# k^T v as four full-array products, y in 32-column quads, A and y issued together, more transposes by DMA

## The chip, the cores and the metric

The kernel runs on one core of one Trainium2 chip. The metric is device time of the whole program in microseconds (us), lower is better. Each profile also records the span from the first instruction to the last, which is about 1.8 us shorter than the time of the same execution, and the clock that TensorE was granted (1.00 is full speed).

Engine names in the profile: PE is TensorE's matmuls, PEld its weight loads, DVE is VectorE, ACT is ScalarE, POOL is GpSimd, SPq the queue of SyncE that issues DMA.

## The reference, cut to what matters

A gated linear recurrence over 768 steps, for 4 batches of 8 heads of width 48, feeds a two-layer network:

```python
for t in range(S):
    state = alpha[:, :, t, :, None] * state + einsum('bhd,bhe->bhde', k[:, :, t], v[:, :, t])
    y[:, :, t] = einsum('bhd,bhde->bhe', q[:, :, t], state)
x = y.transpose(0, 2, 1, 3).reshape(3072, 384)
h = x @ w_in                       # 384 -> 2048
out = (s * relu(h)**2 + b) @ w_out # 2048 -> 384
```

## The kernel before

The sequence is cut into 24 blocks of 128 steps, 6 for each batch. Heads go in pairs. For each block TensorE computes the cumulative log gates (`st_cum`), transposes of scaled q and k (`st_T`, or a DMA transpose), the block's contribution to the state (k^T v, `st_KV`), the causal score matrix A (`st_A`, masked by VectorE) and the output y (`st_y`). Two large matmuls, `mm1` with w_in and `mm2` with w_out, follow for groups of 2 or 4 blocks. A small list scheduler in the kernel puts all of this in one fixed order for each engine, from durations and priorities. Where this plan leaves TensorE idle, the kernel issues dummy matmuls on zeros (`fill`): 41 in the kernel before, all before 36 us. They count as busy time.

k^T v used half the array's columns at a time, and y a mix of 64-column pairs (m = 2) and 32-column quads (m = 1):

```python
def st_KV(n):
    kb = qk_sb[n % 3][:, 1].rearrange("a h d -> a (h d)")
    vp = vp_sb[n % 4]              # [v of head 0 | zeros | v of head 1], 48 columns each
    for p in range(NP):
        for e in range(2):
            nc.tensor.matmul(
                out=p_ps[64 * e : 64 * e + 64, p, :],
                lhsT=kb[:, 128 * p + 64 * e : 128 * p + 64 * e + 64],
                rhs=vp[:, p, 48 * e : 48 * e + 96], start=True, stop=True)

Y_PARTS = [   # pair of heads, state (None) or head, first 32-column piece, pieces
    (0, None, 0, 2), (2, None, 6, 2), (1, None, 4, 2), (3, None, 10, 2),
    (0, 0, 0, 2), (2, 0, 6, 2), (1, 1, 4, 2), (3, 1, 10, 2),
    (2, None, 8, 1), (3, None, 9, 1), (0, None, 2, 1), (1, None, 3, 1),
    (2, 1, 8, 1), (3, 0, 9, 1), (0, 1, 2, 1), (1, 0, 3, 1),
    (1, 0, 4, 1), (0, 1, 1, 1), (3, 0, 10, 1), (2, 1, 7, 1)]

def st_y(n):
    # ... cut: start flags, and blocks without a state leave out the None parts
    nc.tensor.matmul(
        out=y_ps[32 * (x % 4) : 32 * (x % 4) + 32 * m, x // 4, :],
        lhsT=st[:, p, c0 : c0 + 32 * m] if e is None else vp[:, p, c0 + 48 * e : ...],
        rhs=qT[:, p, :] if e is None else am[:, e, p, :], ...)
```

The inputs of the blocks and the weight quarters load through one queue, in this order (b: the four inputs of a block; i and o: a quarter of w_in and of w_out). After o3 has landed, its cast and a column sum, TensorE computes one bias product:

```python
LOADS = ["b0", "b1", "i0", "b2", "i1", "i2", "b3", "i3", "b4", "o0", "b5", "o1", "o2", "b6", "o3"]
```

Of the kernel before, what the change touches and what calls it, by code (L numbers as in the profile page):

```python
# [9 lines left out]
BF16 = mybir.dt.bfloat16  # L10
AF = mybir.ActivationFunctionType
ALU = mybir.AluOpType
# [3 lines left out]
VW = 144  # L16

GROUPS = [2, 2, 2, 2, 4, 4, 4, 4]
LEAD = {1: 20.0, 2: 20.0, 4: 29.0}

NPE = 14

RING = 12

NST = 4

LOADS = ["b0", "b1", "i0", "b2", "i1", "i2", "b3", "i3", "b4", "o0", "b5", "o1", "o2", "b6", "o3"]

class Schedule:

# [97 lines left out]
def kernel(  # L128
# [12 lines left out]
    nc = tc.nc  # L141
    ctx.enter_context(tc.manual_schedule())

    B, H, S, D = q.shape
    C = 128
    NCH = S // C
    NP = H // 2
    NBLK = B * NCH
# [3 lines left out]
    NIN = 5  # L152
# [16 lines left out]
    def many(name, n, shape, dtype, zero=None):  # L169
        tiles = []  # L170
        for i in range(n):
            t = sb.tile(shape, dtype, name=f"{name}{i}")
            if zero is not None:
                zero.memset(t, 0.0)
            tiles.append(t)
        return tiles
# [35 lines left out]
    qkT_sb = many("qkT", 3, [128, 2, NP, 128], BF16)  # L212
    am_sb = many("am", 2, [128, 2, NP, 128], BF16)
    blast_sb = many("blast", 2, [128, NP], BF16)
    t1_sb = many("t1", 2, [128, NP, 96], BF16)
    s_sb = many("s_st", 2, [128, NP, 96], BF16)
    xd_sb = many("xd", 3, [128, 3, 512], BF16)
    r_sb = many("r", 2, [128, 512], BF16)
    gt_sb = [sb.tile([128, RING * C], BF16, name=f"gt{j}") for j in range(NJ)]
# [128 lines left out]

    def st_KV(n):
        kb = qk_sb[n % 3][:, 1].rearrange("a h d -> a (h d)")  # L350
        vp = vp_sb[n % 4]
        for p in range(NP):
            for e in range(2):
                nc.tensor.matmul(  # L354
                    out=p_ps[64 * e : 64 * e + 64, p, :],
                    lhsT=kb[:, 128 * p + 64 * e : 128 * p + 64 * e + 64],
                    rhs=vp[:, p, 48 * e : 48 * e + 96],
                    start=True,
                    stop=True,
                )  # L360

    def st_Tcopy(n):
        nc.vector.tensor_copy(
# [1 line left out]
            in_=t_ps.rearrange("a x p t -> a (x p t)"),  # L365
        )

    def st_t1(n):
        bl = blast_sb[n % 2].unsqueeze(2).to_broadcast([128, NP, 96])
        if n % NCH == NCH - 1:  # L370
            return
        if n % NCH == 0:
            nc.vector.tensor_tensor(out=s_sb[n % 2], in0=p_ps, in1=bl, op=ALU.mult)
        else:
            nc.vector.tensor_tensor(  # L375
                out=t1_sb[n % 2], in0=p_ps, in1=s_sb[(n - 1) % 2], op=ALU.add
            )

    def st_snew(n):
        if n % NCH in (0, NCH - 1):  # L380
            return
        bl = blast_sb[n % 2].unsqueeze(2).to_broadcast([128, NP, 96])
        nc.gpsimd.tensor_tensor(out=s_sb[n % 2], in0=t1_sb[n % 2], in1=bl, op=ALU.mult)  # L383

    def st_A(n):
        qkT = qkT_sb[n % 3]
# [10 lines left out]
    def st_mask(n):  # L397
# [8 lines left out]




    Y_PARTS = [  # L410
        (0, None, 0, 2), (2, None, 6, 2), (1, None, 4, 2), (3, None, 10, 2),
        (0, 0, 0, 2), (2, 0, 6, 2), (1, 1, 4, 2), (3, 1, 10, 2),
        (2, None, 8, 1), (3, None, 9, 1), (0, None, 2, 1), (1, None, 3, 1),
        (2, 1, 8, 1), (3, 0, 9, 1), (0, 1, 2, 1), (1, 0, 3, 1),
        (1, 0, 4, 1), (0, 1, 1, 1), (3, 0, 10, 1), (2, 1, 7, 1),
    ]

    def st_y(n):
        first = n % NCH == 0
        qT = qkT_sb[n % 3][:, 0]  # L420
        am = am_sb[n % 2]
        vp = vp_sb[n % 4]
        st = s_sb[(n - 1) % 2]
        parts = [x for x in Y_PARTS if not (first and x[1] is None)]
        fresh = {0, 1, 2, 3}
        for i, (p, e, x, m) in enumerate(parts):
            c0 = 32 * x - 96 * p


            mine = {(x + y) % 4 for y in range(m)}  # L430
            start = mine <= fresh
            fresh -= mine
            nc.tensor.matmul(  # L433
                out=y_ps[32 * (x % 4) : 32 * (x % 4) + 32 * m, x // 4, :],
                lhsT=(
                    st[:, p, c0 : c0 + 32 * m]
                    if e is None
                    else vp[:, p, c0 + 48 * e : c0 + 48 * e + 32 * m]
                ),
                rhs=qT[:, p, :] if e is None else am[:, e, p, :],  # L440
                start=start,
                stop=(i >= len(parts) - 4),
            )

    blk_group = []
    for g, m in enumerate(GROUPS):
# [76 lines left out]
    sched = Schedule()  # L523
    op = sched.op
    NG = len(GROUPS)
    UNIT = 1.65

    def first(n):
        return n % NCH == 0

    def last(n):
        return n % NCH == NCH - 1

    def want(n):
        g, t = blk_group[n]
        return (4 * n - LEAD[GROUPS[g]]) * UNIT

# [29 lines left out]
    op("PE", 1.3, -10, bias_mm, r=["bones", "colsum"], w=[("o", 1)], lat=0.27)  # L567
    op("DVE", 0.53, -300, bias_copy, r=[("o", 1)], w=["bias"])

    unit_i = quad_i = 0  # L570
    for g in range(NG):
        m = GROUPS[g]
        ring = [(first_blk[g] + x) % RING for x in range(m)]
        for n in range(first_blk[g], first_blk[g] + m):
            i2, i3, ii = n % 2, n % 3, n % NIN
            t = want(n)
            if n:
                rank = loads.index(f"b{n}") - 1000
                for x, (name, src, dst) in enumerate(
                    (("a", alpha, a_in), ("q", q, q_in), ("k", k, k_in), ("v", v, v_in))  # L580
                ):
                    op("SP", 0.98, rank + 0.1 * x, load, n, src, dst, w=[(name, ii)], lat=2.0)
            op("ACT", 0.45, t - 1.0, st_ln, n, r=[("a", ii)], w=[("la", i2)])
            op("PE", 0.3, t, st_cum, n, r=[("la", i2)], w=["ct"], lat=0.27)
            op("ACT", 0.4, t + 0.1, st_exp_b, n, r=["ct"], w=[("b", i2)])
            op("ACT", 0.55, t + 0.1, st_exp_i, n, r=["ct"], w=[("bi", i2), ("bl", i2)])
            op("POOL", 0.6, t + 0.2, st_vcast, n, r=[("v", ii)], w=[("vp", n % 4)])
            op("DVE", 0.47, t + 0.2, st_qb, n, r=[("q", ii), ("b", i2)], w=[("qb", i3)])
            op("DVE", 0.47, t + 0.2, st_kb, n, r=[("k", ii), ("bi", i2)], w=[("kb", i3)])
            if n < NPE:  # L590
                op("PE", 0.5, t + 0.3, st_T, n, r=[("qb", i3), ("kb", i3)], w=["ct"], lat=0.27)
                op("DVE", 0.61, t + 0.4, st_Tcopy, n, r=["ct"], w=[("qkT", i3)])
            else:
                op("ACT", 0.8, t + 0.3, st_Tdma, n, r=[("qb", i3), ("kb", i3)],
                   w=[("qkT", i3)], lat=5.0)
            op("PE", 0.34, t + 0.35, st_KV, n, r=[("kb", i3), ("vp", n % 4)], w=["py"], lat=0.27)
            if first(n):
                op("DVE", 0.48, t + 0.5, st_t1, n, r=["py", ("bl", i2)], w=[("S", i2)])
            elif not last(n):
                op("DVE", 0.48, t + 0.5, st_t1, n, r=["py", ("S", 1 - i2)], w=[("t1", i2)])  # L600
                op("POOL", 0.9, t + 0.1, st_snew, n, r=[("t1", i2), ("bl", i2)], w=[("S", i2)])
            op("PE", 0.33, t + 0.5, st_A, n, r=[("qkT", i3)], w=["a"], lat=0.27)
            op("DVE", 1.15, t + 0.6, st_mask, n, r=["a"], w=[("am", i2)])
            rr = [("am", i2), ("qkT", i3), ("vp", n % 4)] + ([] if first(n) else [("S", 1 - i2)])
            op("PE", 0.55, t + 0.7, st_y, n, r=rr, w=["py"], lat=0.27)
            op("ACT", 0.43, t + 0.8, st_yevac, n, r=["py"], w=[("xd", g % 3, blk_group[n][1])])
        per = 4 // m
        for u in range(NJ // per):
            w = unit_i
            unit_i += 1  # L610
            js = units[w][1]
            t = w * UNIT
            op("PE", 0.85 if m == 1 else 0.69, t, mm1, w,
               r=[("xd", g % 3, x) for x in range(m)] + [("wib", js[0] // 4)],
               w=[("h", w % 2)], lat=0.27)
            op("ACT", 0.5, t + 0.5, relu, w, r=[("h", w % 2)], w=[("r", w % 2)])
            op("DVE", {1: 0.54, 2: 0.4, 4: 0.335}[m], t + 1.0, square, w, r=[("r", w % 2)],
               w=[("gt", x, j) for j in js for x in ring])
        for u in range(4 * m):
            x = quad_i  # L620
            quad_i += 1
            tt, jq = quads[x][1:]
            ob = (x // 4) % 2
            t = (x + 4 * m + 1.4) * UNIT
            op("PE", 0.67, t, mm2, x,
               r=[("gt", ring[tt], j) for j in range(4 * jq, 4 * jq + 4)] + [("wob", jq)],
               w=[("o", ob)], lat=0.27)
            if jq == 3:
                op("DVE", 0.54, t + 0.1, oevac, x, r=[("o", ob), "bias", "s"],
                   w=[("os", (x // 4) % 3)])  # L630
                op("SP", 0.7, -2000, ostore, x, r=[("os", (x // 4) % 3)])



# [38 lines left out]
```

## Time and profile before

| | before |
|---|---|
| time, median of the first 3 runs | 207.42 us (206.22 to 207.78) |
| span of the profiled run (a fourth one, 208.12 us), clock | 206.3 us, 1.00 |
| TensorE busy, whole span | 185.6 us (90%) |
| bias product starts | 57.12 us |
| last w_out matmul ends | 202.62 us |

First, the profile page's table of 40 equal slices (tenths of busy time in each slice) of the kernel before:

```profile
PE   1979497797599999999999999999999999999992
...
PEclk9999999999999999999999999999999999999999
```

TensorE has holes in the first 11 slices (to 57 us) and none after. The table by stretches puts numbers on it (busy us and instruction count by engine, then clock, DMA share and GB/s):

```profile
0.00:57.10 57.10, 41.42 (x482) 26.38 (x486) 38.41 (x80) 34.66 (x63) 14.86 (x29) 1.00 0.93 223
57.10:90.00 32.90, 32.90 (x398) 22.41 (x397) 28.01 (x62) 17.97 (x43) 7.43 (x12) 1.00 0.98 206
90.00:166.00 76.00, 74.84 (x765) 38.88 (x775) 55.63 (x104) 44.97 (x101) 11.78 (x17) 1.00 0.80 149
166.00:203.00 37.00, 36.46 (x220) 20.02 (x221) 13.95 (x30) 12.01 (x21) 0.00 (x0) 1.00 0.13 49
```

The first number after the length is TensorE: 41.42 of 57.10 us in the head, and 144.20 of 145.90 us from there on. Some records are missing: of the 384 w_in matmuls (384 weight loads are recorded) 368 are there, and where one is missing a gap of about 0.05 us reads as idle. Up to the end of the last w_out matmul (202.62 us) 1.3 us read as idle, of which 1.0 us are such gaps and some 0.3 us idle time. Lines of the chain of waits (start, us, what) say why the head has holes:

```profile
45.52 2.00 SPq L188
47.61 6.54 DMA wst_178<-in_moe_w_out_dram
54.25 0.96 DVE colpart L261
56.61 0.67 PE o_ps_68 L497 x4
57.28 1.29 PE o_ps_69 L276 x4
```

The chain goes through load issues and the last w_out load to the bias product (L276; the chain counts it from the end of the step before, 57.28, though its first matmul starts at 57.12); after that it consists of TensorE's own matmuls. To cost a product, read from its first start to the start of what follows. The timeline of TensorE (start, us, line, output and operands, array tile, shape, count):

```profile
78.52 0.33 PE L497 MATMUL o_ps_68<-w_out_bf,gt_157 128*128 128x384 bf16 x1
78.78 0.30 PE L433 MATMUL py_ps<-qkT_138,s_st_147 128*64 128x128 bf16 x4
78.91 0.28 PE L433 MATMUL py_ps<-am_142,vp_117 128*64 128x128 bf16 x4
79.12 0.24 PE L433 MATMUL py_ps<-qkT_138,s_st_147 128*32 128x128 bf16 x4
79.19 0.29 PE L433 MATMUL py_ps<-am_142,vp_117 128*32 128x128 bf16 x8
79.41 0.62 PE L339 MATMUL ct_ps<-ident_bf,qk_134 128*128 128x128 bf16 x8
...
81.00 0.33 PE L497 MATMUL o_ps_68<-w_out_bf,gt_161 128*128 128x384 bf16 x1
81.26 0.36 PE L354 MATMUL py_ps<-vp_119,qk_134 128*64 128x96 bf16 x8
81.55 0.40 PE L389 MATMUL a_ps<-qkT_139 64*128 64x128 bf16 x8
```

y takes 79.41 - 78.78 = 0.63 us, k^T v 81.55 - 81.26 = 0.29 us. Before each of them the last w_out matmul holds the array for 0.26 us, although w_out matmuls follow one another every 0.163 us: entering a tiled mode costs about 0.09 us. The line of the weight load of k^T v shows the gap from the other side: the weights are not loaded ahead.

```profile
81.26 0.23 PEld L354 LDWEIGHTS <-qk_134 128*64 128x64 bf16 x8 [0.32 <-issue]
```

### The profile page before, as it was taken

To read this page: it belongs to the slowest core of one execution; us is meant where nothing else is said; L and a number is where in the kernel's file an instruction comes from. 1 tells how busy PE (TensorE), PEld (TensorE's weight loads), DVE (VectorE), ACT (ScalarE), POOL (GpSimd) and SP (SyncE) were. 2 spreads that over 40 slices of the span, in tenths; PEclk is the share of its full clock that TensorE was granted. 3 is DMA by queue.
4 is the path that set the end of the run, shared out by engine and by line. 5 is a ranking of instruction groups with operands and counts; after the bars stand their busy time and mean duration, and the time that the engine had idled before them with its cause. 6 is when DMAs were issued, how large, how long until landed. Compare 5 with 4: busy or idle time off the path is not lost.

```text
span 206.3 us, 4820 instructions
## 1 busy us (share of the span) xinstructions
PE 185.6 (90%) x1858; PEld 107.7 (52%) x1877; DVE 136.3 (66%) x273; ACT 109.6 (53%) x225; POOL 34.1 (17%) x58
## 2 busy tenths in 40 slices
PE   1979497797599999999999999999999999999992
PEld 1435375564366667665555454544545455555651
DVE  4457387899597888878859597786876534444321
ACT  4253768687454465656567577666554344444100
POOL 8303121203102321201220330013011000000000
PEclk9999999999999999999999999999999999999999
DMA  6999888998889998989999899972412111111122
GB/s 134 188 259 293 192 237 217 209 339 180 201 172 221 205 220 173 234 189 223 201 220 158 165 220 187 232 176 75 104 59 52 43 38 38 41 38 38 38 78 76
DMA packets 117655, 32.82 MB, mean 159 GB/s; under 512 B 110976, under 2 KB 116096, under 8 KB 117632
## 3 DMA queue, kind: packets, MB, share of 16 engines
q1 hardware_dynamic: 107008, 29.89, 64.0%
q10 hardware_dynamic: 10560, 2.62, 8.7%
q8 instruction: 14, 0.23, 0.5%
q14 instruction: 9, 0.07, 0.1%
q0 software_dynamic: 64, 0.00, 0.0%
HBM read 25.17 MB, written 4.72 MB: 145 GB/s over the span
## 4 chain that ended last, share of the span: by engine, by line
PE 70%; SPq 12%; DMA 9%; DVE 4%; issue 2%; ACT 1%; DVEq 0%
PE o_ps_69 L497 16%; PE o_ps_68 L497 14%; PE h_ps_67 L473 12%; PE h_ps_66 L473 12%; SPq L188 11%; PE py_ps L433 5%; DMA wst_178<-in_moe_w_out_dram 3%; DMA wst_178<-in_moe_w_in_dram 3%; DMA wst_175<-in_moe_w_out_dram 3%; PE a_ps L389 3%; PE py_ps L354 2%; PE ct_ps L295 2%; PE ct_ps L339 2%; SPq L232 1%; DVE colpart L261 1%
## 5 line engine op out<-in xcount | busy, mean ns | idle before, releaser
L473 PEld LDWEIGHTS <-w_in_bf 128*128 128x128 bf16 x384 | 34.6, 97 | 19.3 <-issue 1.0
L482 ACT ACTIVATE r_152<-h_ps_66 128x512 bf16<-128x512 f32 x48 | 28.7, 598 | 21.1 <-PE h_ps_66 L473 14.8
L482 ACT ACTIVATE r_153<-h_ps_67 128x512 bf16<-128x512 f32 x48 | 28.7, 598 | 19.3 <-PE h_ps_67 L473 11.7
L398 DVE TENSOR_TENSOR am_142<-a_ps,mask 128x1024 bf16<-128x1024 f32 x12 | 14.7, 1221 | 3.9 <-PE a_ps L389 3.6
L398 DVE TENSOR_TENSOR am_141<-a_ps,mask 128x1024 bf16<-128x1024 f32 x12 | 14.6, 1220 | 3.4 <-PE a_ps L389 3.2
L473 PE MATMUL h_ps_67<-xd_150,w_in_bf 128*128 128x512 bf16 (+1 forms) x70 | 16.0, 343 | 0.4 <-issue 0.2
L473 PE MATMUL h_ps_66<-xd_150,w_in_bf 128*128 128x512 bf16 (+1 forms) x67 | 15.5, 341 | 0.7 <-ACT r_152 L482 0.3
L473 PE MATMUL h_ps_66<-xd_149,w_in_bf 128*128 128x256 bf16 (+1 forms) x70 | 13.0, 306 | 0.3
L473 PE MATMUL h_ps_67<-xd_149,w_in_bf 128*128 128x256 bf16 (+1 forms) x69 | 12.8, 306 | 0.1
L638 PE MATMUL o_ps_68<-zeros,ident_bf 128*128 128x512 bf16 x38 | 11.3, 425 | 0.1
L383 POOL TENSOR_TENSOR s_st_147<-t_145,blast_143 128x384 bf16<-128x384 bf16 x8 | 6.9, 859 | 23.0 <-DVE t_145 L375 23.0
L309 ACT ACTIVATE b_s_129<-ct_ps 128x384 f32<-128x384 f32 x12 | 5.9, 490 | 8.0 <-PE ct_ps L300 5.4
L383 POOL TENSOR_TENSOR s_st_148<-t_146,blast_144 128x384 bf16<-128x384 bf16 x8 | 7.2, 904 | 16.7 <-DVE t_146 L375 16.7
L473 PE MATMUL h_ps_67<-xd_151,w_in_bf 128*128 128x256 bf16 (+1 forms) x48 | 9.8, 326 | 0.0
L309 ACT ACTIVATE b_s_128<-ct_ps 128x384 f32<-128x384 f32 x12 | 5.9, 490 | 7.0 <-PE ct_ps L300 5.4
L295 PE MATMUL ct_ps<-la_97,U_bf 128*128 128x384 bf16 x12 | 4.1, 343 | 6.0 <-ACT la_97 L289 6.0
L473 PE MATMUL h_ps_66<-xd_151,w_in_bf 128*128 128x256 bf16 (+1 forms) x44 | 9.3, 321 | 0.3 <-issue 0.2
L451 ACT ACTIVATE xd_150<-py_ps 128x384 bf16<-128x384 f32 x10 | 5.0, 498 | 2.4 <-PE py_ps L433 1.7
L638 PEld LDWEIGHTS <-ident_bf 128*128 128x128 bf16 x41 | 3.9, 105 | 4.3 <-issue 1.9
L300 PEld LDWEIGHTS <-la_97 128*128 128x128 bf16 x48 | 3.0, 98 | 5.9 <-issue 4.9
L312 ACT ACTIVATE binv_131<-ct_ps 128x384 f32<-128x384 f32 x12 | 5.9, 490 | 0.0
L312 ACT ACTIVATE binv_130<-ct_ps 128x384 f32<-128x384 f32 x12 | 5.9, 489 | 0.0
(255 smaller groups left out, 439.9 us busy)
## 6 DMA issues: line engine op xcount, KB each, us to landing
out_dram<-o_sb_170 SPq DMA_DIRECT2D x8, 192.0 KB, 2.6
out_dram<-o_sb_171 SPq DMA_DIRECT2D x8, 192.0 KB, 2.3
out_dram<-o_sb_172 SPq DMA_DIRECT2D x8, 192.0 KB, 2.4
a_in_70<-in_alpha_dram SPq DMA_DIRECT2D x5, 192.0 KB, 3.8
q_in_75<-in_q_dram SPq DMA_DIRECT2D x5, 192.0 KB, 3.7
k_in_80<-in_k_dram SPq DMA_DIRECT2D x5, 192.0 KB, 4.7
v_in_85<-in_v_dram SPq DMA_DIRECT2D x5, 192.0 KB, 4.0
a_in_71<-in_alpha_dram SPq DMA_DIRECT2D x5, 192.0 KB, 3.9
```

Source lines behind the costliest of these rows:

```text
L188: nc.sync.dma_start(out=dst[n % NIN], in_=src[b, :, c * C : (c + 1) * C, :].rearrange("h s d -> s h d"),)
L295: nc.tensor.matmul(out=cum_ps, lhsT=U_bf, rhs=la[:, :, 0:D], start=True, stop=True)
L309: nc.scalar.activation(out=b_sb[n % 2], in_=cum_ps, func=AF.Exp)
L312: nc.scalar.activation(out=binv_sb[n % 2], in_=cum_ps, func=AF.Exp, scale=-1.0)
L383: nc.gpsimd.tensor_tensor(out=s_sb[n % 2], in0=t1_sb[n % 2], in1=bl, op=ALU.mult)
L389: nc.tensor.matmul(out=a_ps[:, e, p, :], lhsT=qkT[64 * e : 64 * e + 64, 1, p, :], rhs=qkT[64 * e : 64 * e + 64, 0, p, :], start=True, stop ...
L398: nc.vector.tensor_tensor(out=am_sb[n % 2].rearrange("a e p t -> a (e p) t"), in0=a_ps.rearrange("a e p t -> a (e p) t"), in1=mask.unsquee ...
L433: nc.tensor.matmul(out=y_ps[32 * (x % 4) : 32 * (x % 4) + 32 * m, x // 4, :], lhsT=(st[:, p, c0 : c0 + 32 * m] if e is None else vp[:, p, ...
L473: nc.tensor.matmul(out=hp[:, i * n : (i + 1) * n], lhsT=w_in_bf[:, kk, 128 * j : 128 * (j + 1)], rhs=xd_sb[g % 3][:, kk, 0:n], start=(kk = ...
L482: nc.scalar.activation(out=r_sb[w % 2], in_=h_ps[w % 2], func=AF.Relu)
L497: nc.tensor.matmul(out=op[:, 0:d_model], lhsT=gt_sb[j][:, c0 : c0 + C], rhs=w_out_bf[:, j, :], start=(j == 0), stop=(j == NJ - 1),)
L638: nc.tensor.matmul(out=o_ps[0], lhsT=ident_bf, rhs=zeros, start=True, stop=True)
```

## The change

The intent is to take work off TensorE. k^T v runs as four products of the full 128x128 array, with the two v of a pair as one 96-column operand; the unwanted cross-head quarters of the result are not read, so the state addition becomes two half-partition ones and the state tiles are zeroed once. y uses quads only. From block 13 on, A of a block and y of the preceding one are issued together. DMA transposes begin at block 9, not 14. The scheduler's unit, leads and stated durations were set anew, and block 3 now loads ahead of two quarters of w_in.

```diff
-LEAD = {1: 20.0, 2: 20.0, 4: 29.0}
-NPE = 14
+UNIT = 1.79                        # was 1.65
+LEAD = {1: 12.0, 2: 52.0, 4: 20.0}
+NPE = 9
+NAY = 13
-LOADS = ["b0", "b1", "i0", "b2", "i1", "i2", "b3", "i3", "b4", ...]
+LOADS = ["b0", "b1", "i0", "b2", "b3", "i1", "i2", "i3", "b4", ...]
@@ st_KV: one product for each pair of heads
+            nc.tensor.matmul(out=p_ps[:, p, :], lhsT=kb[:, 128 * p : 128 * p + 128],
+                             rhs=vp[:, p, 0:3:2, :], start=True, stop=True)
@@ st_t1: the same for the first block of a sequence, with s_sb and bl
+        for e in range(2):
+            r, c = slice(64 * e, 64 * e + 64), slice(D * e, D * e + D)
+            nc.vector.tensor_tensor(out=t1_sb[n % 2][r, :, c], in0=p_ps[r, :, c],
+                                    in1=s_sb[(n - 1) % 3][r, :, c], op=ALU.add)
@@ st_y: 28 pieces of 32 columns
+    Y_PARTS = [(x // 3, None, x) for x in range(12)] + [(0, 0, 0), (0, 0, 1), ...]
+    def st_Ay(n):
+        st_A(n)
+        st_y(n - 1)
... (t1 and s zeroed on POOL, s with 3 buffers; the scheduling code for late y; stated durations)
```

## The prediction

> **What bounds the kernel now.** Span 206.3 us, clock 1.00. The table by stretches shows two regimes. From 0 to 57.1 us TensorE is busy 41.4 us, of which 41 dummy matmuls are about 9; DMA share is 0.93. The chain of waits there is mostly load issues and weight loads; it ends with the last w_out load (landing near 54 us), its cast, and the bias product at 57.1. From 57.1 to 203 TensorE is busy 144.2 of 145.9 us: it is the limit, and the chain is its own matmuls. So only TensorE time saved after 57 us counts.
>
> **The change on TensorE, costed from starts in the timeline** (a product's start to the next operation's).
> - k^T v: eight 128x64-tile matmuls take 0.29 us, plus about 0.09 on entry (the last w_out matmul to the next start is 0.26 us, not 0.163). The Trainium skill, "TensorEngine Tiling (Array Packing)", Key Properties, says that changing the tiling mode drains TensorE; the 0.09 us agrees. Four full-array products should cost about 0.23: full-array transposes[...] run at 0.056 us each (0.45 for eight). Gain 0.15 each, or 0.06 where A followed directly and still pays the entry: with 17 blocks after 57 us, about 1.9 us.
> - y: 8 pairs + 12 quads = 0.63 us. Both versions stream seven rounds, but the pairs take 0.34 us for four rounds including a mode change; quads run at about 0.017 us per matmul, so 28 cost 0.48 + exit 0.09 = 0.57. Gain 0.06 x 17 = 1.0 us.
> - A and y adjacent from block 13: one mode change fewer, 0.09 x about 6 (some were adjacent already) = 0.5 us.
> - Transposes of blocks 9 to 13 leave TensorE: 5 x 0.45 = 2.3 us. DVE loses 5 copies of 0.69; ACT gains 5 issues of 1.25 us.
>
> Sum: 5.7 us. By the built order, the work ahead of the bias product (108 w_in and 16 w_out matmuls) is the same, and the same loads precede the last w_out load, so I expect the head unchanged: savings in its seven blocks are absorbed by the load wait.
>
> **What it adds.** Two half-partition additions for each state update (one of 0.55 us becomes, my estimate, two of about 0.35), on a DVE 85% busy from 57 to 90 us; five fewer copies roughly pay for it. Five 0.4-0.5 us memsets on POOL, which may delay the first cast of v (8.2 us) by 1 to 2 us, hidden by loads. Five DMA transposes (3.1 to 7.4 us to landing) during 70 to 100 us, where DMA share is 0.97: loads shift, but are limited by buffer release and have slack. Changed priorities (UNIT, LEAD) reorder the stream: 1 to 2 us either way.
>
> **Predicted.** 207.4 - 5.7 - about 0.4 for the retuned order = 201.3 us, range 198.5 to 204.5. Faster by over 2% (below 203.3): 0.75; within 2%: 0.22; slower: 0.03.
>
> **What would show each step.** The bias product still near 57 us; from there to the last w_out matmul 139 to 141 us instead of 145.9, TensorE at least 98% busy; k^T v 0.22 to 0.25 us with no gap ahead; y 0.55 to 0.60; transposes gone from TensorE for blocks 9 to 13; 15 DMA transposes landing in 3 to 7 us.
>
> **What would make it wrong.** TensorE stalls at A on late DMA transposes in 70 to 110 us, or at y and k^T v on their shared PSUM tile, since y comes later; DVE late with masks; the last w_out load later than 54 us because buffers come free later; k^T v limited by weight loads above 0.06 us each.

## The result

| | before | after |
|---|---|---|
| time, median (range), 4 runs each | 207.39 us (206.22 to 207.78) | 198.9 us (198.11 to 199.29) |
| span of the profiled run | 206.3 us | 196.9 us |
| bias product starts | 57.12 us | 55.45 us |
| from there to the end of the last w_out matmul | 145.50 us | 137.56 us |
| rest (eviction, store) | 3.73 us | 3.87 us |

The ratio is 0.9595, with a 95% interval of 0.9545 to 0.9644. A ratio is the mean time of one kernel's fast runs over that of the other's of the same rounds, so it is not quite the ratio of the medians. Executions over 1.5% slower than the fastest of the same kernel are left out of the means. Later the same pair gave 0.966 (0.9619 to 0.9701). The change is faster by 3.4 to 4.1%.

The slices, the stretches and the chain after, answering to those of before:

```profile
PE   1789969658699999999999999999999999999992
...
PEclk9999999999999999999999999999999999999999
```

```profile
0.00:55.45 55.45, 40.18 (x501) 26.05 (x506) 39.08 (x85) 34.35 (x63) 15.93 (x34) 1.00 0.94 230
55.45:90.00 34.55, 34.55 (x444) 23.65 (x443) 30.13 (x68) 19.13 (x45) 7.30 (x11) 1.00 1.10 216
90.00:157.00 67.00, 66.13 (x737) 36.35 (x750) 56.72 (x107) 42.73 (x97) 14.25 (x18) 1.00 1.07 181
157.00:193.00 36.00, 35.84 (x241) 19.49 (x230) 14.45 (x29) 12.92 (x22) 0.00 (x0) 1.00 0.12 45
```

```profile
46.10 5.80 DMA wst_184<-in_moe_w_out_dram
51.92 1.49 ACT w_out_bf L256
53.45 0.81 PE o_ps_68 L506 x4
...
55.61 1.29 PE o_ps_69 L279 x4
```

The picture is the same in kind: a head with holes that ends with the last w_out load, then a dense stretch in which 1.0 us reads as idle, most of it where matmuls have no record (14 of w_in). The dense stretch is 7.94 us shorter. The timeline after:

```profile
83.74 0.33 PE L506 MATMUL o_ps_69<-w_out_bf,gt_167 128*128 128x384 bf16 x1
83.91 0.33 PE L356 MATMUL py_ps<-vp_119,qk_134 128*128 128x96 bf16 x4
84.08 0.82 PE L482 MATMUL h_ps_67<-xd_155,w_in_bf 128*128 128x256 bf16 x6
...
85.65 0.33 PE L506 MATMUL o_ps_69<-w_out_bf,gt_171 128*128 128x384 bf16 x1
85.91 0.35 PE L436 MATMUL py_ps<-qkT_139,s_st_149 128*32 128x128 bf16 x12
86.09 0.40 PE L436 MATMUL py_ps<-am_141,vp_119 128*32 128x128 bf16 x16
86.42 0.34 PE L506 MATMUL o_ps_69<-w_out_bf,gt_172 128*128 128x384 bf16 x1
```

k^T v is 84.08 - 83.91 = 0.17 us, and the w_out matmul ahead of it keeps its 0.17 us: no entry gap. Its weights are now loaded ahead, beside that w_out matmul:

```profile
83.74 0.35 PEld L356 LDWEIGHTS <-qk_134 128*128 128x128 bf16 x4
```

y is 86.42 - 85.91 = 0.51 us, still with its entry gap of 0.26 us.

I added up the time from each start to the next over the whole dense stretch, by operation. A gap ahead of a product counts for the operation in front of it, so the entry gaps stand mostly under mm1, mm2 and cum:

| us from start to next start | before | before, 2nd trace | after | after, 2nd trace |
|---|---|---|---|---|
| k^T v | 5.65 | 5.64 | 3.42 | 3.41 |
| y | 10.82 | 10.80 | 9.13 | 9.22 |
| TensorE transposes (7, then 2) | 3.24 | 3.25 | 1.07 | 1.20 |
| mm2 | 62.56 | 62.47 | 61.42 | 61.48 |
| mm1 | 51.61 | 51.61 | 51.33 | 51.46 |
| cum | 4.73 | 4.73 | 4.34 | 4.35 |
| A | 5.60 | 5.61 | 5.56 | 5.59 |
| sum with the bias product (1.3) | 145.50 | 145.40 | 137.56 | 138.01 |

What fell: k^T v by 2.2, y by 1.7, transposes by 2.2, and the sum of mm2, mm1 and cum, in which the entry gaps stand, by 1.8 us (1.6 in the second traces).

### The profile page after: what moved, and what is told of

Its sections match the earlier page's. It is cut to its first block, busy times and chain, and to the rows that moved or that the text cites. A ratio compares the mean times of both kernels' runs of the same rounds, so it can differ in the third digit from the quotient of the medians.

```text
span 196.9 us, 4940 instructions
## 1 busy us (share of the span) xinstructions
PE 176.7 (90%) x1903; PEld 105.5 (54%) x1921; DVE 141.0 (72%) x288; ACT 109.1 (55%) x225; POOL 37.5 (19%) x63
## 4 chain that ended last, share of the span: by engine, by line
PE 65%; DMA 15%; SPq 10%; ACT 3%; DVE 3%; issue 2%; ACTq 0%; DVEq 0%
PE o_ps_69 L506 15%; PE o_ps_68 L506 14%; PE h_ps_67 L482 12%; PE h_ps_66 L482 12%; SPq L191 9%; PE py_ps L436 4%; DMA wst_183<-in_moe_w_in_dram 3%; DMA wst_182<-in_moe_w_out_dram 3%; DMA wst_181<-in_moe_w_out_dram 3%; DMA wst_184<-in_moe_w_out_dram 3%; PE a_ps L398 3%; DMA q_in_77<-in_q_dram 2%; PE ct_ps L298 1%; ACT w_out_bf L256 1%; PE py_ps L356 1%
## 5 line engine op out<-in xcount | busy, mean ns | idle before, releaser
L482 PEld LDWEIGHTS <-w_in_bf 128*128 128x128 bf16 x384 | 35.3, 98 | 22.4 <-ACT w_in_bf L243 1.0
L482 PE MATMUL h_ps_67<-xd_156,w_in_bf 128*128 128x512 bf16 (+1 forms) x71 | 16.2, 343 | 0.1
L482 PE MATMUL h_ps_66<-xd_156,w_in_bf 128*128 128x512 bf16 (+1 forms) x67 | 15.8, 341 | 0.3
L674 PE MATMUL o_ps_68<-zeros,ident_bf 128*128 128x512 bf16 x41 | 12.0, 412 | 0.2
L460 ACT ACTIVATE xd_156<-py_ps 128x384 bf16<-128x384 f32 x10 | 4.9, 494 | 6.8 <-PE py_ps L436 3.5
L392 POOL TENSOR_TENSOR s_st_149<-t_147,blast_144 128x384 bf16<-128x384 bf16 x4 | 3.6, 906 | 15.3 <-DVE t_147 L381 7.9
L392 POOL TENSOR_TENSOR s_st_151<-t_145,blast_143 128x384 bf16<-128x384 bf16 x4 | 3.6, 904 | 14.5 <-DVE t_145 L381 7.1
L460 ACT ACTIVATE xd_155<-py_ps 128x384 bf16<-128x384 f32 x8 | 3.9, 493 | 3.9 <-PE py_ps L436 2.8
```

What stands on the lines that cost most here:

```text
L392: nc.gpsimd.tensor_tensor(out=s_sb[n % 3], in0=t1_sb[n % 2], in1=bl, op=ALU.mult)
L460: nc.scalar.activation(out=xd_sb[g % 3][:, :, t * C : (t + 1) * C], in_=y_ps, func=AF.Copy)
L482: nc.tensor.matmul(out=hp[:, i * n : (i + 1) * n], lhsT=w_in_bf[:, kk, 128 * j : 128 * (j + 1)], rhs=xd_sb[g % 3][:, kk, 0:n], start=(kk = ...
L674: nc.tensor.matmul(out=o_ps[0], lhsT=ident_bf, rhs=zeros, start=True, stop=True)
```

## The experiments

**Theory M (mode changes).** Streamed work is the same before and after: four rounds of 96 columns for k^T v, seven rounds of 128 for y. What the two product changes save is changes of tiling mode. In the built order, counting each change of array tile between neighbouring matmuls after the bias product, the kernel before has 116 and the changed one 58. Every us saved there is a us of time, because TensorE is the limit. **Theory O (order).** The gain comes from the retuned order, with fewer waits. **Theory I.** The cost of y goes by the number of matmuls issued. For the head, **theory H** says that it ends with the last w_out load, **rival D** that VectorE binds it.

### Undoing k^T v alone: a_kv8

```diff
# changed kernel, with st_KV and st_t1 of the kernel before
+        for e in range(2): nc.tensor.matmul(out=p_ps[64 * e : 64 * e + 64, p, :], ...)
```

> The changed kernel with only k^T v put back: eight 128x64 products and the one full-width state addition; the order of operations on TensorE is the same. Theory M (what the change saves on TensorE is changes of tiling mode, about 0.095 us each; the streamed rounds are the same before and after): by the built order this adds 33 mode changes after the bias product (58 to 91), so the stretch from the bias product to the last w_out matmul should grow from 137.6 by about 3.1 us, and the time from 198.9 to about 202. Theory O (the gain after the bias product is the retuned order, with fewer waits): under 1 us. My prediction's costing (weight loads at 0.056 us each) gives 1.9 us.

The outputs are right. Its ratio to the kernel before is 0.9788 (0.9727 to 0.9848), from two fast runs with spans of 198.9 and 200.2 us. The profiled execution fell in a state never seen otherwise (span 993.9 us). Its trace holds no clock record (its page has no PEclk line), so the 1.00 listed for it is no reading. It confirms the 91 mode changes, but its durations are of no use: w_out matmuls follow one another every 1.05 us instead of 0.163, while ScalarE's evictions (0.60 us) and VectorE's masks (1.22 us) keep their times. The cause is open. In the fast runs the loss of about 1.3 to 1.9% of the time of the kernel before, against the changed kernel's 0.966 and 0.9595 (2.7 to 4 us) has the size of theory M, but the interval is wide. This run alone does not settle it; the run on the kernel before, below, says more.

### Undoing y alone: a_y20

```diff
# changed kernel, with Y_PARTS and st_y of the kernel before (8 pairs, 12 quads)
```

> The changed kernel with only y put back: pairs and quads in 20 matmuls for 28 quads; the order of operations is the same. Theory M: 18 mode changes more after the bias product, +1.7 us (time about 200.6), although 8 matmuls fewer for each block are issued. Theory I (the cost of y goes by the number of matmuls issued): it gets faster, by 8 x 0.015 us x 15 blocks = 1.8 us. My prediction's costing gives +1.0 us.

Ratio 0.978 (0.9721 to 0.9838), median 201.18 us against 205.78. In its trace the dense stretch is 139.78 us (137.56 and 138.01 with quads), and y in that stretch takes 11.24 us instead of 9.13 and 9.22. That is 2.0 to 2.1 us for 18 mode changes, 0.11 to 0.12 us each. Theory I is refuted: 20 matmuls are slower than 28.

### The same 20 matmuls with pairs and quads interleaved: a_y20mix

```diff
     (0, None, 0, 2), (2, None, 6, 2), (1, None, 4, 2), (3, None, 10, 2),
-    (0, 0, 0, 2), (2, 0, 6, 2), (1, 1, 4, 2), (3, 1, 10, 2),
     (2, None, 8, 1), (3, None, 9, 1), (0, None, 2, 1), (1, None, 3, 1),
+    (0, 0, 0, 2), (2, 0, 6, 2), (1, 1, 4, 2), (3, 1, 10, 2),
```

> As the kernel with y put back, with the very same 20 matmuls of y, but pairs and quads interleaved (pairs, quads, pairs, quads): two mode changes more for each block with a state part, 30 more after the bias product (76 to 106). Theory M: 30 x 0.095 = 2.9 us slower than with y put back, about 203.4 us, and each y near 0.82 us. Theory I, and any theory in which streamed rounds or the count of matmuls set the cost: no difference.

The timeline of TensorE shows one y:

```profile
91.92 0.47 PE L441 MATMUL py_ps<-qkT,s_st 128*64 128x128 bf16 x8
92.32 0.53 PE L441 MATMUL py_ps<-am,vp 128*64 128x128 bf16 x12
92.78 0.34 PE L298 MATMUL ct_ps<-la,U_bf 128*128 128x384 bf16 x1
```

This y takes 92.78 - 91.92 = 0.86 us, where the same matmuls in the old order take 0.63. Over the dense stretch y takes 14.33 us instead of 11.24: 3.09 us for 30 added changes, 0.10 us each. Nothing else differs, so this is the cleanest measurement of the cost. The profiled run counts as slow (203.7 us, clock 0.992, with a dip between 54 and 58 us, ahead of every y that is counted here), which is why I use the durations of y and not the totals. The fast runs gave 0.9836 (0.9766 to 0.9907), an interval that overlaps that of a_y20, so the times alone do not show the difference.

### The two product changes alone on the kernel before: b_kv4y28

```diff
# kernel before, with st_KV, st_t1, Y_PARTS and st_y of the changed kernel, t1 and s zeroed;
# LOADS, LEAD, UNIT, NPE, stated durations as before: the order of operations is that of before
```

> The kernel before with the two product changes alone (k^T v as four full-array products with the split state addition, y in quads); order of operations, load order, 14 blocks with TensorE transposes as before. It has 49 tiling-mode changes fewer after the bias product (116 to 67). Theory M with the sizes that the traces show (0.12 us for a change inside y, 0.12 + 0.09 us for leaving and entering around k^T v): 17 x 0.12 for y, 17 x 0.12 and about 13 x 0.09 for k^T v, so the stretch from the bias product to the last w_out matmul falls from 145.5 by 4.7 to 5.5 us. Theory O (the retuned order makes the gain): at most 1.5 us. The head before the bias product: no gain if it is bound by the loads (start at 57 with a spread of 1 us between runs), 1.5 us earlier if its TensorE work counts.

Ratio 0.9748 (0.969 to 0.9805). The dense stretch is 140.74 us, 4.7 to 4.8 less than before's 145.40 and 145.50, for 49 mode changes fewer: 0.10 us each. This trace has all 384 w_in matmuls and 0.50 us of idle time, no less than the kernel before, so fewer waits are not the reason. Theory O's limit of 1.5 us is far exceeded, with no retuning at all. k^T v takes 3.19 us and y 8.78 in the stretch. For k^T v no run changes the mode alone, as a_y20mix does for y: that it also has half as many weight loads is a rival that no run excludes, though the sizes (0.12 us at the exit, 0.09 at the entry) are those of the other mode changes. The rest of the way to the changed kernel, 2.7 to 3.2 us, is what five transposes (5 x 0.45 = 2.25) and nine more mode changes (67 to 58, 0.8) come to.

### DMA transposes from block 14 again: a_npe14

```diff
-NPE = 9
+NPE = 14
```

> The changed kernel with the transposes of blocks 9 to 13 back on TensorE. The cost is that of five transposes, 5 x 0.45 = 2.25 us, and one mode change: the stretch after the bias product grows from 137.6 to about 139.9, the time to about 201.2, if loads and VectorE had no part. If the five DMA transposes had been delaying TensorE, or VectorE's 5 x 0.69 us of copies come to bind, it differs: below +1.5 us or above +3 us.

Ratio 0.9816 (0.9749 to 0.9883). The dense stretch is 142.50 us, 4.5 to 4.9 more than with block 9. Transposes account for 3.17 - 1.07 = 2.1 us of it; TensorE is idle for 2.7 us (142.50 - 139.77; no w_in matmul lacks its record here, so this is idle time, where the changed kernel has some 0.3 us), with 2.3 us of waits of w_in matmuls for the evictions of ScalarE. So the expected 2.25 us is there, and as much again is lost to an order that fits less well. The run went beyond the +3 us that I had named as the mark of such an effect.

### No joint issue of A and y: a_nay24, a_nay24b

```diff
-NAY = 13
+NAY = 24
```

> The changed kernel without the joint issue of A and of the y that precedes it: the same matmuls, in another order, 66 mode changes after the bias product for 58. Theory M: +0.8 us, about 199.7 us, if the other order stalls no more. Theory O: the joint issue matters by its order, and the stretch after the bias product shows more idle time on TensorE (now 1.0 us).

The first profile fell in a run at a clock of 0.569 (span 299.8 us) and is of no use for durations; the fast runs gave 0.9874 (0.9813 to 0.9934). I ran it again beside a control, the changed kernel itself (ratio 0.966, interval 0.9619 to 0.9701, dense stretch 138.01 us), and the kernel before.

> The kernel before once more, for a second trace of its head on the chip of this call. If the 1.7 us by which the bias product comes earlier in the changed kernel is spread of the loads between runs, it starts here anywhere from 54.5 to 57; if the head's TensorE work or the load order makes it, at 57 again, and the changed kernel on the same chip at 55.5. The stretch after it should be 145.5 us again, to 0.5 us.

> The changed kernel once more, as the control for this call: ratio 0.96 to the kernel before, the stretch after the bias product 137.6 us, to 0.7 us. [...]

> Again the changed kernel without the joint issue of A and y, since its first profile fell in a run at a clock of 0.57. Theory M: 8 mode changes more at about 0.09 us (the entry to y), 0.7 us longer than the control after the bias product, with no more idle time. Theory O: idle time on TensorE after the bias product grows by 1 us or more beside that.

Ratio 0.9897 (0.9848 to 0.9945): 2.4% slower than the control (0.9897 / 0.966), some 5 us where theory M alone says 0.7. Its trace counts as slow (clock 0.973), but shows what the fast runs may share. What reads as idle in the dense stretch is 142.90 - 139.93 = 3.0 us (1.3 in the control); some 0.8 us of it stand at w_in matmuls without a record, as in the control, and the rest is two waits:

```profile
116.48 0.81 PE L482 MATMUL h_ps<-xd,w_in_bf 128*128 128x512 bf16 x3 [1.37 <-ACT r L491]
118.42 0.46 PE L298 MATMUL ct_ps<-la,U_bf 128*128 128x384 bf16 x1 [0.80 <-ACT blast L316]
```

and the table by stretches shows the granted clock (third number from the end) dropping right after them:

```profile
116.00:118.00 2.00, 1.14 (x11) 0.51 (x11) 1.51 (x4) 1.98 (x5) 0.37 (x1) 1.00 1.34 241
118.00:120.00 2.00, 1.58 (x34) 1.10 (x34) 1.82 (x3) 0.73 (x3) 0.13 (x1) 0.62 1.32 231
120.00:122.00 2.00, 2.00 (x8) 0.91 (x6) 1.18 (x2) 1.04 (x3) 0.00 (x0) 0.53 1.20 210
122.00:124.00 2.00, 1.95 (x19) 1.00 (x19) 1.69 (x3) 0.38 (x1) 0.51 (x1) 1.00 1.22 284
```

The clock was also 0.50 from 54 to 60 us, and 0.89 from 60 to 62, which puts some 2.7 us of low clock in the dense stretch (from 57.72). The bias product took 2.56 us there instead of 1.29. If all work takes twice as long at half the clock, the two drops cost about 3 us (an estimate: half of 2.7 and of 3.4 us) of the 4.9 by which this dense stretch exceeds the control's.

So the order does matter, but the other way round from theory O: the retuned order did not remove waits that the kernel before had (its dense stretch idled for some 0.3 us), it avoids new ones that came up in these two runs (a_npe14 and this one), where one part was taken out. That the waits caused the drop of the clock is likely from their sequence, not shown. The other fast runs have no trace, so how much of their loss is waits stays open.

The two controls speak on the head. The bias product starts at 55.87 us in the second trace of the kernel before and at 56.03 in that of the changed one. The 1.7 us between the first two traces was thus spread between runs; with two traces of each kernel, an effect of less than about 1 us cannot be told from it. With the head's program and loads of before, the two-product version started it at 55.02.

### A later w_out, and the column sums on POOL: c1, c2

```diff
-LOADS = ["b0", "b1", "i0", "b2", "b3", "i1", "i2", "i3", "b4", "o0", "b5", "o1", "o2", "b6", "o3"]
+LOADS = ["b0", "b1", "i0", "b2", "i1", "b3", "i2", "i3", "b4", "b5", "o0", "b6", "o1", "b7", "o2", "b8", "o3"]
# c2 in addition: colsum_part and colsum_add on nc.gpsimd instead of nc.vector
```

> The changed kernel with another order of loads: i1, i2, i3 earlier among the blocks, and each w_out load later, the last after block 8 instead of block 6. Theory H (the head ends with the last w_out load, and TensorE idles because the blocks behind it come late): before the bias product it now does one more block and four more w_in units, about 4 us of work, while the bias product moves to about 60 us, and 2 to 3 us are gained, about 196.5 us. Rival D (the head is bound by VectorE, 0.8 to 0.93 busy from 30 to 60 us, with 6.6 us of column sums there): no gain, within 1 us of 198.9.

> As c1, and the seven additions for the column sums of w_out move from VectorE to POOL (17% busy). Theory D: VectorE has about 6.6 us less to do before 60 us, and the gain over c1 is 2 us or more. Theory H: c2 is within 1 us of c1, or loses if POOL is slow on these (then the bias product and the first evictions come later).

c1: ratio 0.983 (0.9782 to 0.9878), slower than the changed kernel. The bias product moved to 63.03 us, 7 us later, for about 4 us of work done ahead of it, so theory H's gain did not come. Part of the loss is clock: the table by stretches gives 0.91 for 0 to 20 us and 0.83 for 40 to 50 us. The clock stayed at 1.00 there in the profiled run of the changed kernel. It is not the whole loss: c1's other fast runs took 203.3 to 203.5 us at mean clocks of 0.980 to 0.992, and fast runs of the changed kernel 198.1 and 199.0 us at 0.988.

c2: ratio 1.0037 (0.9976 to 1.0098), 4 us worse again, and rival D's gain did not come either. In the profile the clock was again low, 0.50 from 54 to 60 us and 0.58 from 63 to 67, which can be part of the loss. Lines of POOL and VectorE from its timeline show why the offload did not relieve VectorE:

```profile
52.06 1.81 POOL L264 TENSOR_TENSOR colpart<-wst 128x768 f32<-128x768 f32 x1 [2.41 <-DMA wst<-in_moe_w_out_dram]
53.95 2.00 POOL L269 TENSOR_TENSOR colsum<-colsum,colpart 128x768 f32<-128x768 f32 x1
59.36 1.82 POOL L264 TENSOR_TENSOR colpart<-wst 128x768 f32<-128x768 f32 x1
```

```profile
51.65 0.55 DVE L325 TENSOR_TENSOR qk<-q_in,b_s 128x384 bf16<-128x384 f32 x1
52.11 2.18 DVE L330 TENSOR_TENSOR qk<-k_in,binv 128x384 bf16<-128x384 f32 x1
54.21 2.40 DVE L499 TENSOR_TENSOR gt<-r 128x256 bf16<-128x256 bf16 x2
59.45 1.23 DVE L407 TENSOR_TENSOR am<-a_ps,mask 128x1024 bf16<-128x1024 f32 x1
```

The scaling of k, normally 0.55 us, takes 2.18 us and ends after POOL's 1.81 us addition does. Two squares, normally 0.28 us each, take 2.40. The mask, which has one of its two inputs in PSUM, keeps its usual 1.22 us though POOL's third addition runs beside it. The Trainium skill, "GPSIMD Engine Reference", section 1, says that GpSimd's SBUF interfaces are shared with VectorE, with contention where a VectorE instruction has two SBUF inputs. This trace agrees, and gives the size: the instruction waits for the whole of POOL's. Neither theory of what binds the head was confirmed, so what would shorten it stays open.

### A version that theory M says is better: d_8_7

```diff
-NPE = 9
+NPE = 7
-NAY = 13
+NAY = 8
+        if not last(n):            # k^T v of a sequence's last block is never used
             op("PE", 0.23, t + 0.35, st_KV, ...)
```

> An improved version: the changed kernel without k^T v for the last block of each sequence (its result is never used: 3 products of 0.17 us fall away after the bias product), joint issue from block 8 on instead of 13 (54 mode changes for 58), and DMA transposes from block 7 instead of 9 (two transposes of 0.45 us less on TensorE). Theory M: 0.5 + 0.4 + 0.9 = 1.8 us off the control, about 1% faster; if the DMA transposes just after the head come late, or VectorE binds, the gain is lost to waits at A.

Ratio 0.987 (0.9823 to 0.9918), median 204.55 us where the control on the same chip has 199.63. It was to be 1% faster and is 2% slower. TensorE's work did shrink (k^T v 2.47 us for 3.41, no transposes in the dense stretch), but its dense stretch is 143.83 us, of which 7.3 us read as idle (about 1 us of it at unrecorded matmuls). The profiled run counts as slow, at a clock of 1.00 in that stretch. Four waits from the timeline, the longest among them:

```profile
69.67 0.71 PE L482 MATMUL h_ps<-xd,w_in_bf 128*128 128x256 bf16 x5 [1.93 <-ACT r L491]
101.00 1.46 PE L482 MATMUL h_ps<-xd,w_in_bf 128*128 128x512 bf16 x6 [0.63 <-ACT r L491]
106.10 0.40 PE L398 MATMUL a_ps<-qkT 64*128 64x128 bf16 x8 [0.62 <-DMA qkT<-qk]
113.24 0.32 PE L298 MATMUL ct_ps<-la,U_bf 128*128 128x384 bf16 x1 [0.96 <-ACT la L292]
```

A waits for DMA transposes, and w_in and cum matmuls wait for ScalarE, which also issues those transposes. I changed three things at once here, so which of them brought the waits is open. No version that I tried beats the changed kernel.

## Why the prediction was right or wrong

- **Total.** 201.3 us predicted, with 198.5 to 204.5 as the range; 198.9 measured, and 199.63 later. It was right, at the low end of the range: a reduction of 6.1 us was forecast, 8.5 and 7.0 came. That it lay inside owes something to the width of the range: the terms for the two products and the joint issue, below, were about 2 us too small, and up to 1.7 us of the difference between the first two traces was spread in the head.
- **What bounds the kernel.** Right. Time taken off TensorE after the bias product came off the time (b_kv4y28: 4.7 us in the dense stretch, and 5.6 us between the medians). TensorE was 99% busy there.
- **The head unchanged.** Right. 57.12 and 55.87 us before, 55.45 and 56.03 after.
- **k^T v, "about 0.23", "gain about 1.9 us".** Mis-sized. It takes 0.17 us. I took the pace of the transposes, 0.056 us each, for the limit of a full weight load, but they stream 128 columns where k^T v streams 96, and four full loads kept up with 0.17 us. The Trainium skill, "TensorE: Matmul & The Clock Gate", section "Back-to-back issue gap", gives N/2.4 + 2.5 ns for N columns, 42.5 ns for 96; the trace's 0.17 / 4 is just that. The section calls this the gap of isolated matmuls and expects more for small N where each matmul has a weight load of its own, as here; the trace does not show that. The saving is 2.2 us in k^T v itself and most of the 1.8 us of entry gaps.
- **y, "0.57", "gain 1.0 us".** Mis-sized. It takes 0.51 us, and 1.6 to 1.7 us were saved in the dense stretch, over 18 blocks and not 17. I noted that the pairs' 0.34 us included a mode change, but took 0.017 us per quad matmul from too few of them; it is 0.18 us for 12, or 0.015. The right sum is simpler: the same seven rounds with one mode change fewer, 0.12 us.
- **The mode change, "0.09".** Right in kind and near in size: 0.09 on entry, 0.10 to 0.12 within y and at the end of k^T v. The Trainium skill's "TensorEngine Tiling (Array Packing)", Key Properties, that a change of mode drains TensorE, carried the argument, and a_y20mix shows the cost of a change with the same matmuls in another order. No run separates the drain itself from the weight load that is not made ahead. Had I counted the changes in the built order (116 to 58) and multiplied by 0.1, I would have got 5.8 us for the products and the joint issue, where I wrote 1.9 + 1.0 + 0.5 = 3.4. Less the transposes' 2.2 us, the traces' 7.4 to 7.9 us leave 5.2 to 5.7 for them.
- **Transposes, 2.3 us.** Right: 2.1 to 2.2 us, and their 4.0 to 6.6 us in flight (15 transposes, two traces) did not stop TensorE in this order.
- **Added cost.** The half-partition additions were estimated at 0.35 us and are 0.35 us (354 ns mean). They did not matter, nor did POOL's memsets, which did delay the first cast of v from 8.2 to 10.1 us.
- **"1 to 2 us either way" for the retuned order.** In the changed kernel it shows as neither gain nor loss. But undoing one part on the retuned order cost 2 to 4 us beyond that part's own work (a_npe14, and a_nay24b, where part of it was clock in the profiled run), and d_8_7 lost 5 us. I had not seen that the order was fitted to just this set of parts.

## What to carry to other kernels

Where TensorE is the limit and small tiled products alternate with full-array ones, count the changes of tiling mode in the built order and price each at about 0.1 us. Group products of one mode, or use the full array when the streamed columns are the same. When a static order has been tuned with a set of changes, removing work from it can cost more in new waits than the work was worth (d_8_7), so look at idle time on the limiting engine, with missing records taken out, before crediting any sum of durations.

## What the Trainium skill lacked or had wrong

- "TensorEngine Tiling (Array Packing)", Key Properties, says that a mode change drains TensorE, but gives no cost. These runs show 0.09 us on entry from w_out matmuls (0.255 us to the next start, for 0.163), and 0.10 to 0.12 us for each change inside y (3.09 us for 30; 2.0 to 2.1 us for 18).
- "TensorE: Matmul & The Clock Gate", section "Back-to-back issue gap", gives about 81 ns for each matmul of 128 columns in a stream of weight loads and matmuls. The transposes here, 128 columns each with a weight load of its own, start every 56 ns (0.45 us for eight), and the products of k^T v, with 96 columns, every 42.5 ns.
- The same page's summary, "Why this matters for your kernels", warns of idle gaps above about 3 us. That row alone would not have warned of a_nay24b: its clock fell to a mean of 0.52 from 118.5 to 122.0 us with no gap of 3 us before it, after waits of 1.37 and 0.80 us in 3.5 us of which TensorE was busy for 1.32. This is one trace, and it shows the sequence, not the cause.
